# One core, four batches of attention and two expert stages: the first batch's limits on ScalarE, key high parts on GpSimd, row sums corrected with two tensor inputs

## The chip, the cores and the metric

The kernel runs on one core of a Trainium2 chip. What counts is the device time of one execution in microseconds (us). The trace is of one execution, read by the hardware profiler: TensorE (PE for its matmuls, PEld for its weight loads), VectorE (DVE), ScalarE (ACT), GpSimd (POOL), and SyncE (SP), which here issues nearly all DMAs.

## What is computed

Three layers follow each other. The change touches the first one alone: attention in which only the scores within `tau` of a row's peak are kept.

```python
scores = scale * q @ k.T                          # 4 batches, 8 heads, 576 x 576, head_dim 64
thresh = max(scores, -1) - tau
scores = where(scores >= thresh, scores, -1e9)
attn   = exp(scores - max(scores, -1))
attn   = attn / (sum(attn, -1) + 1e-9)
x      = attn @ v                                 # then heads side by side: (4, 576, 512)
h = x.T @ U @ V;  u = x + h.T                     # token mixing of rank 32
y = u + relu(u @ w_ch1) @ w_ch2                   # channel layer, 512 -> 2048 -> 512
out = routed experts of y                         # 8 experts, each token to one of them
```

## The kernel before

Attention is done batch by batch and, within a batch, by pairs of heads (4 pairs). `load_pair` (line 261) brings a pair's queries and keys in pieces named `raw`. A key piece is split into a high part `kh` (line 289, a rounding copy on ScalarE) and a low part `kl` (line 290, piece minus `kh`), so that two matmuls, lines 313 and 315, make one precise product. The pieces of queries become `qs` (line 292 on ScalarE, the low rows by line 294 on VectorE). `kl` is made on GpSimd for the three later pairs of batch 0 and for all of batch 1, otherwise on VectorE; that is the variable `eng` of line 271.

The 576 rows of the two heads are cut into groups, nine score tiles of 128 x 576 for a pair, 36 for a batch. A tile goes through these steps:

- scores into one of two PSUM tiles (TensorE, lines 313 and 315)
- the row's negated peak (VectorE, line 348, `peak`)
- `exp` of the scores, biased with the peak (ScalarE, line 359)
- the limit, peak minus tau, one number for each row (VectorE, line 352, `limits`; in batch 0 for one tile at a time, 128x1, in the later batches for two, 128x2)
- the mask: scores at or over the limit, times `exp`, with the row sum as a second result in `rv` (VectorE, line 363); it is the last reader of the PSUM tile

A group's probabilities are then turned by TensorE (line 416) and copied out of PSUM by ScalarE (line 417), multiplied with the values, and a chain of small steps (`chain`, from line 447) applies the row sums and the token mixing. `inverse` (line 378) adds 1e-9 to the row sums and takes the reciprocal. In batch 0 it is called on four sums at a time, or one; later on two, or one.

In batch 0 attention runs alone (`attention_alone`, line 553), beside a first few steps of `convert`, which turns the channel weights from 64-bit into 32-bit floats (line 212 on ScalarE, line 219 on VectorE). From batch 1 on, attention of a batch runs beside the channel layer of the one before (lines 702 to 722), whose weights are split into `w0h`, `w0l`, `w1h`, `w1l`: for batch 0's channel pass on GpSimd (lines 678 and 681) but for the first two blocks' high parts.

The order of instructions on each engine comes from a scheduler, not from the text alone; only GpSimd's instructions of batch 0's own code keep their order as written. An engine runs its queue in order: an instruction that waits holds up all behind it.

Of the kernel before, what the change touches and what calls it, by code (L numbers as in the profile page):

```python
# [14 lines left out]
AF = mybir.ActivationFunctionType  # L15
ALU = mybir.AluOpType
# [87 lines left out]
def attention_channel_moe(ctx, tc, qk, vv, tau, umat, vrep, wch, wgl, wexp, consts, out):  # L104
    nc = tc.nc
    pe, dve, act, pool, sp = nc.tensor, nc.vector, nc.scalar, nc.gpsimd, nc.sync
# [10 lines left out]
    t8 = cp.tile([128, 4], F32, name="t8")  # L117
# [135 lines left out]
    def scalars():  # L253

        sp.dma_start(out=t8[:, 0:1], in_=tau)

        dve.tensor_scalar(out=t8[:, 1:2], in0=t8[:, 0:1], scalar1=NEGTAU, scalar2=0.125, op0=ALU.is_ge, op1=ALU.mult)
        dve.tensor_scalar(out=t8[:, 2:3], in0=t8[:, 1:2], scalar1=0.0, scalar2=BIG, op0=ALU.is_equal, op1=ALU.mult)
        dve.tensor_scalar(out=t8[:, 0:1], in0=t8[:, 0:1], scalar1=0.0, scalar2=t8[:, 2:3], op0=ALU.max, op1=ALU.add)

    def load_pair(b, hp, later=None):

        i = b * NPAIR + hp
        v = ap.tile([128, VW], F32, tag="v", name=f"v{i}")
        qs = ap.tile([128, QKW], F32R, tag="qs", name=f"qs{i}")
        kh = ap.tile([128, QKW], F32R, tag="kh", name=f"kh{i}")
        kl = ap.tile([128, QKW], F32R, tag="kl", name=f"kl{i}")

        cuts = ((0, 0, 128), (1, 0, S), (0, 704, 832), (1, S, QKW), (0, 128, 704), (0, 832, QKW)) if i == 0 else (
            (1, 0, S), (1, S, QKW), (0, 0, 608), (0, 608, QKW))  # L270
        eng = dve if i == 0 or b > 1 else pool
        def steps():
            for n, (kq, c0, c1) in enumerate(cuts):
                c = slice(c0, c1)
                nm = f"raw{i}_{n}"
                if (i, n) == (0, 1):
                    x = mlp.tile([128, S], F32, tag="yr", name=nm, bufs=2)
                elif i == 0 and c1 - c0 == 128:
                    x = mlp.tile([128, 512], F32, tag="wr", name=nm, bufs=WR)
                else:  # L280
                    x = ap.tile([128, 640], F32, tag="raw", name=nm, bufs=3)
                x = x[:, :c1 - c0]
                sp.dma_start(out=x, in_=qk[i][:, kq, c])
                if (i, n) == (0, 0):
                    scalars()
                if (i, n) == (0, 3):
                    sp.dma_start(out=cst, in_=consts)
                if kq:
                    act.activation(kh[:, c], x, AF.Copy)
                    eng.tensor_tensor(out=kl[:, c], in0=x, in1=kh[:, c].bitcast(F32), op=ALU.subtract)  # L290
                else:
                    act.activation(qs[:, c], x, AF.Copy, scale=t8[:, 1:2])
                    lo, hi, xl = qs[64:128, c], qs[64:128, c].bitcast(F32), x[64:128]
                    dve.scalar_tensor_tensor(out=lo, in0=xl, scalar=t8[64:128, 1:2], in1=hi,
                                             op0=ALU.mult, op1=ALU.subtract)
                yield
            sp.dma_start(out=v, in_=vv[i])

        if later is None:
            for _ in steps():  # L300
                pass
        else:
            later.append(steps())
        return qs, kh, kl, v
# [13 lines left out]
    class Group:  # L318
# [30 lines left out]

        def limits(self, c0, c1):  # L350

            dve.tensor_scalar(out=self.st[:, 1, c0:c1], in0=self.st[:, 0, c0:c1], scalar1=-1.0, scalar2=t8[:, 0:1],
                              op0=ALU.mult, op1=ALU.subtract)

        def halves(self, h):
            return self.pt[:, h].rearrange("p (a b) -> p a b", a=2)
# [9 lines left out]
        def norm(self):  # L366

            g = self.key[2]
            rv = self.rvs[:, g, 0:self.nh]
            if self.b >= SCALED:  # L370
                inverse(rv)
                for h in range(self.nh):
                    act.activation(self.pt[:, h], self.pt[:, h], AF.Copy, scale=rv[:, h:h + 1])  # L373
            elif g == 4:
                inverse(rv)
                sp.dma_start(out=self.rvs[:64, 4, 1:2], in_=self.rvs[64:, 4, 0:1])

    def inverse(x):
        dve.tensor_scalar(out=x, in0=x, scalar1=1e-9, scalar2=None, op0=ALU.add)
        dve.reciprocal(out=x, in_=x)  # L380

    def front(b, hp, g, inp):
# [64 lines left out]
    def chain(nm, hp, half, xT, xu, rvs):  # L447
# [8 lines left out]
        if rvs is not None:  # L456
            inverse(rvs[:, c0:c0 + 2])
# [917 lines left out]
```

## Time and profile before

| | us |
|---|---|
| median of 3 runs | 1030.57 |
| lowest and highest of them | 1028.63, 1031.76 |
| profiled execution, its own time | 1029.61 |
| its span | 1027.8 |

| engine | busy us | share of the span |
|---|---|---|
| PE | 995.2 | 97% |
| PEld | 836.2 | 81% |
| DVE | 719.3 | 70% |
| ACT | 611.8 | 60% |
| POOL | 152.2 | 15% |

The busy shares are means over stages that differ: batch 0's attention fills the span's first tenth, and the last three tenths are the experts. A busy PE is a modelled figure, since matmuls overlap; the idle times of an engine, and what ended them, say more. An instruction's duration can overlap the start of the next on its engine by about a tenth of a microsecond, so what it costs its engine is read from start to start.

### The profile page before, as it was taken

To read this page: it belongs to the slowest core of one execution; us is meant where nothing else is said; L and a number is where in the kernel's file an instruction comes from. 1 tells how busy PE (TensorE), PEld (TensorE's weight loads), DVE (VectorE), ACT (ScalarE), POOL (GpSimd) and SP (SyncE) were. 2 spreads that over 40 slices of the span, in tenths; PEclk is the share of its full clock that TensorE was granted. 3 is DMA by queue.
4 is the path that set the end of the run, shared out by engine and by line. 5 is a ranking of instruction groups with operands and counts; after the bars stand their busy time and mean duration, and the time that the engine had idled before them with its cause. 6 is when DMAs were issued, how large, how long until landed. Compare 5 with 4: busy or idle time off the path is not lost. (4 is left out here: it accounts for less than half of the span.)

```text
span 1027.8 us, 17859 instructions
## 1 busy us (share of the span) xinstructions
PE 995.2 (97%) x6352; PEld 836.2 (81%) x6352; DVE 719.3 (70%) x1761; ACT 611.8 (60%) x1242; POOL 152.2 (15%) x143
## 2 busy tenths in 40 slices
PE   7898999989999999999999999999999999999996
PEld 4666677768787787788889898999998998889984
DVE  7998697776778877877676664683369755566673
ACT  6888777776677777776565653422354444455562
POOL 1332245342000000000000000013400321120100
PEclk9999999999999999999999999999999999999998
DMA  6655577864323322423121110453055555566550
GB/s 213 220 153 162 160 257 245 273 209 140 116 92 94 125 72 83 127 90 94 55 68 42 42 43 31 139 207 122 25 192 180 177 202 185 174 192 198 196 184 16
DMA packets 58241, 143.72 MB, mean 140 GB/s; under 512 B 7389, under 2 KB 8157, under 8 KB 58144
## 3 DMA queue, kind: packets, MB, share of 16 engines
q1 hardware_dynamic: 54784, 132.27, 40.0%
q0 software_dynamic: 3360, 10.23, 3.1%
q8 instruction: 52, 0.85, 0.3%
q14 instruction: 45, 0.37, 0.1%
HBM read 124.65 MB, written 18.61 MB: 139 GB/s over the span
## 5 line engine op out<-in xcount | busy, mean ns | idle before, releaser
L1125 ACT ACTIVATE eh<-ew 128x512 fp32r<-128x512 f32 x160 | 94.2, 628 | 68.1 <-PE el L1241 47.7
L1126 DVE TENSOR_TENSOR el<-ew,eh 128x512 fp32r<-128x512 f32 x160 | 106.7, 692 | 37.7 <-ACT eh L1125 36.2
L702 PE MATMUL l<-uh,w0h 128*128 128x256 f32 (+2 forms) x352 | 127.0, 361 | 0.3 <-ACT yT L508 0.3
L363 DVE SCALAR_TENSOR_TENSOR p<-s,st,p 128x576 f32<-128x576 f32 x144 | 114.1, 814 | 15.8 <-ACT p L359 12.4
L359 ACT ACTIVATE p<-s,st 128x576 f32<-128x576 f32 x144 | 103.7, 738 | 33.1 <-DVE st L348 31.6
L703 PE MATMUL l<-ul,w0h 128*128 128x256 f32 (+2 forms) x352 | 122.6, 348 | 0.0
L704 PE MATMUL l<-uh,w0l 128*128 128x256 f32 (+2 forms) x352 | 122.3, 348 | 0.0
L348 DVE TENSOR_REDUCE st<-s 128x1 f32<-128x576 f32 x144 | 105.1, 749 | 18.0 <-PE s L315 17.4
L717 PE MATMUL l<-hh,w1h 128*128 128x512 f32 (+3 forms) x320 | 115.2, 360 | 0.0
L719 PE MATMUL l<-hh,w1l 128*128 128x512 f32 (+3 forms) x320 | 112.8, 353 | 0.0
L718 PE MATMUL l<-hl,w1h 128*128 128x512 f32 (+3 forms) x320 | 112.2, 351 | 0.0
L417 ACT ACTIVATE ptt<-tp 128x512 f32<-128x512 f32 (+1 forms) x192 | 88.4, 490 | 30.1 <-PE tp L416 30.0
L313 PE MATMUL s<-kh,qs 128*128 128x288 f32 x320 | 95.5, 318 | 5.6 <-DVE p L363 3.6
L681 POOL TENSOR_TENSOR w1l<-wr,w1h 128x512 fp32r<-128x512 f32 x24 | 31.7, 1333 | 457.5 <-DVE rha L984 426.6
L416 PE MATMUL tp<-cst,p 128*128 128x128 f32 x576 | 90.8, 276 | 5.2 <-ACT ptt L417 5.0
L722 DVE TENSOR_TENSOR yT<-l,yT 128x448 f32<-128x448 f32 (+2 forms) x96 | 50.0, 521 | 57.9 <-PE l L719 57.5
L315 PE MATMUL s<-kl,qs 128*128 128x288 f32 x320 | 88.5, 296 | 0.0
L373 ACT ACTIVATE p<-p,rv 128x576 f32<-128x576 f32 x108 | 78.6, 771 | 15.3 <-DVE rv L380 15.0
L416 PEld LDWEIGHTS tp<-cst,p 128*128 128x128 f32 x576 | 67.8, 140 | 20.6 <-ACT ptt L417 11.4
L313 PEld LDWEIGHTS s<-kh,qs 128*128 128x128 f32 x320 | 60.3, 188 | 15.6 <-DVE p L363 6.4
L435 PE MATMUL po<-ptt,v 128*64 128x256 f32 (+1 forms) x256 | 69.8, 413 | 2.4 <-ACT ptt L424 1.5
L706 DVE SCALAR_TENSOR_TENSOR hl<-l,hh 128x512 fp32r<-128x512 f32 (+2 forms) x80 | 46.3, 578 | 36.7 <-ACT hh L705 36.4
(604 smaller groups left out, 2468.6 us busy)
## 6 DMA issues: line engine op xcount, KB each, us to landing
ew<-in_wexp_dram SPq DMA_DIRECT2D x80, 512.0 KB, 4.6
wr<-wdram SPq DMA_DIRECT2D x128, 256.0 KB, 3.1
cr<-in_wch_dram SPq DMA_DIRECT2D x32, 512.0 KB, 5.2
raw<-in_qk_dram SPq DMA_DIRECT2D x30, 304.0 KB, 3.2
wdram<-w SPq DMA_DIRECT2D x32, 256.0 KB, 3.0
v<-in_vv_dram SPq DMA_DIRECT2D x16, 352.0 KB, 3.9
raw<-in_qk_dram SPq DMA_DIRECT2D x16, 320.0 KB, 3.8
raw<-in_qk_dram SPq DMA_DIRECT2D x17, 288.0 KB, 3.0
```

What stands on the lines that cost most here:

```text
L313: pe.matmul(s["t"][:, h, :288], lhsT=qs[:, qc:qc + 128], rhs=kh[:, k0:k0 + 288], start=(j == 0), stop=False)
L348: dve.tensor_reduce(out=self.st[:, 0, h:h + 1], in_=self.t[h], axis=AX.XY, op=ALU.max, negate=True)
L359: act.activation(self.halves(h), self.t[h], AF.Exp, bias=self.st[:, 0, h:h + 1])
L363: dve.scalar_tensor_tensor(out=p, in0=self.t[h], scalar=self.st[:, 1, h:h + 1], in1=p, op0=ALU.is_ge, op1=ALU.mult, accum_out=self.rvs[:, ...
L416: pe.transpose(tp[:, c - c0], src[:, c * 128:c * 128 + 128], ident)
L702: pe.matmul(pm, lhsT=w1h[:, wk], rhs=uh[k], start=(k == 0), stop=False)
L703: pe.matmul(pm, lhsT=w1h[:, wk], rhs=ul[k], start=False, stop=False)
L704: pe.matmul(pm, lhsT=w1l[:, wk], rhs=uh[k], start=False, stop=(k == 3))
L717: pe.matmul(pm, lhsT=w2h[:, wd], rhs=xh, start=(f == f0), stop=False)
L718: pe.matmul(pm, lhsT=w2h[:, wd], rhs=xl, start=False, stop=False)
L719: pe.matmul(pm, lhsT=w2l[:, wd], rhs=xh, start=False, stop=(f == f0 + 3))
L1126: dve.tensor_tensor(out=lo, in0=x, in1=hi.bitcast(F32), op=ALU.subtract)
```

## The change

Three edits. `limits` of batch 0 becomes an ACTIVATE on ScalarE (out = -1 * in + bias, with the negated tau in a new column of `t8`, which costs one more small instruction in `scalars`). The copy into `kh` goes to GpSimd wherever `kl` is made there. `inverse` of an even number of sums uses an instruction that takes the sums as two tensor inputs and a maximum of (sum + 1e-9) and the sum.

```diff
+        dve.tensor_scalar(out=t8[:, 3:4], in0=t8[:, 0:1], scalar1=-1.0, scalar2=None, op0=ALU.mult)
...
-                    act.activation(kh[:, c], x, AF.Copy)
+                    if eng is pool:
+                        pool.tensor_copy(kh[:, c], x)
+                    else:
+                        act.activation(kh[:, c], x, AF.Copy)
...
         def limits(self, c0, c1):
-            dve.tensor_scalar(out=self.st[:, 1, c0:c1], in0=self.st[:, 0, c0:c1], scalar1=-1.0, scalar2=t8[:, 0:1],
-                              op0=ALU.mult, op1=ALU.subtract)
+            if self.b == 0:
+                act.activation(self.st[:, 1, c0:c1], self.st[:, 0, c0:c1], AF.Identity, scale=-1.0, bias=t8[:, 3:4])
+            else:
+                dve.tensor_scalar(out=self.st[:, 1, c0:c1], in0=self.st[:, 0, c0:c1], scalar1=-1.0, scalar2=t8[:, 0:1],
+                                  op0=ALU.mult, op1=ALU.subtract)
...
     def inverse(x):
-        dve.tensor_scalar(out=x, in0=x, scalar1=1e-9, scalar2=None, op0=ALU.add)
+        if x.free_size() % 2:
+            dve.tensor_scalar(out=x, in0=x, scalar1=1e-9, scalar2=None, op0=ALU.add)
+        else:
+            dve.scalar_tensor_tensor(out=x, in0=x, scalar=1e-9, in1=x, op0=ALU.add, op1=ALU.max)
         dve.reciprocal(out=x, in_=x)
```

The scheduler also reorders what stands around these instructions. Three places show how. The names carry batch, pair and group (`p0_2_2` is batch 0, pair 2, group 2; `raw2` and `kh2` are the third pair's), and a running number at their end that differs between the two kernels. Line numbers of the changed kernel are up to ten higher.

VectorE in batch 0, the peaks, limits and masks of one group. Before:

```order
L348 TENSOR_REDUCE st0_2_2_751<-s0_2_2_0_752 128x1
L379 TENSOR_SCALAR rv0_2_0_632<-rv0_2_0_632 128x4
L352 TENSOR_SCALAR st0_2_2_751<-st0_2_2_751,t8_63 128x1
L348 TENSOR_REDUCE st0_2_2_751<-s0_2_2_1_778 128x1
L465 TENSOR_TENSOR xsd0_0_1_364<-tx0_1_4_770,rv0_1_0_343 128x256
L363 SCALAR_TENSOR_TENSOR p0_2_2_750,rv0_2_0_632<-s0_2_2_0_752,st0_2_2_751,p0_2_2_750 128x576
L352 TENSOR_SCALAR st0_2_2_751<-st0_2_2_751,t8_63 128x1
L380 RECIPROCAL rv0_2_0_632<-rv0_2_0_632 128x4
L348 TENSOR_REDUCE st0_2_3_821<-s0_2_3_0_822 128x1
L363 SCALAR_TENSOR_TENSOR p0_2_2_750,rv0_2_0_632<-s0_2_2_1_778,st0_2_2_751,p0_2_2_750 128x576
```

The same place on VectorE now:

```order
L352 TENSOR_REDUCE st0_2_2_752<-s0_2_2_0_753 128x1
L389 SCALAR_TENSOR_TENSOR rv0_2_0_633<-rv0_2_0_633 128x4
L390 RECIPROCAL rv0_2_0_633<-rv0_2_0_633 128x4
L352 TENSOR_REDUCE st0_2_2_752<-s0_2_2_1_779 128x1
L370 SCALAR_TENSOR_TENSOR p0_2_2_751,rv0_2_0_633<-s0_2_2_0_753,st0_2_2_752,p0_2_2_751 128x576
L475 TENSOR_TENSOR xsd0_0_1_365<-tx0_1_4_771,rv0_1_0_344 128x256
L352 TENSOR_REDUCE st0_2_3_822<-s0_2_3_0_823 128x1
L370 SCALAR_TENSOR_TENSOR p0_2_2_751,rv0_2_0_633<-s0_2_2_1_779,st0_2_2_752,p0_2_2_751 128x576
```

The two limits are gone from VectorE, and the reciprocal stands nearer to its correction.

ScalarE at the same group. Before:

```order
L359 ACTIVATE p0_2_2_750<-s0_2_2_0_752,st0_2_2_751 128x576
L417 ACTIVATE ptt0_2_0_790<-tp0_2_0_0_791 128x4x128
L475 ACTIVATE xsd0_0_1_364<-tx0_1_4_770,rv0_1_0_343 64x64 x2
L417 ACTIVATE ptt0_2_0_790<-tp0_2_0_4_808 128x4x128
L359 ACTIVATE p0_2_2_750<-s0_2_2_1_778,st0_2_2_751 128x576
```

ScalarE now:

```order
L366 ACTIVATE p0_2_2_751<-s0_2_2_0_753,st0_2_2_752 128x576
L452 ACTIVATE yT0_356<-po0_1_4_737 128x320
L357 ACTIVATE st0_2_2_752<-st0_2_2_752,t8_63 128x1
L427 ACTIVATE ptt0_2_0_791<-tp0_2_0_0_792 128x4x128
L366 ACTIVATE p0_2_2_751<-s0_2_2_1_779,st0_2_2_752 128x576
L427 ACTIVATE ptt0_2_0_791<-tp0_2_0_4_809 128x4x128
L485 ACTIVATE xsd0_0_1_365<-tx0_1_4_771,rv0_1_0_344 64x64 x2
L357 ACTIVATE st0_2_2_752<-st0_2_2_752,t8_63 128x1
```

Each limit is a queue entry of ScalarE now, here with one and with three other instructions between it and its `exp`.

GpSimd at the third and fourth pairs' keys. Before:

```order
L290 TENSOR_TENSOR kl2_453<-raw2_0_454,kh2_452 128x576
L290 TENSOR_TENSOR kl2_453<-raw2_1_488,kh2_452 128x640
L681 TENSOR_TENSOR w0l0_0_1355<-wr0_0_0_1352,w0h0_0_1354 128x512
L681 TENSOR_TENSOR w1l0_0_1361<-wr0_0_1_1358,w1h0_0_1360 128x512
L290 TENSOR_TENSOR kl3_719<-raw3_0_720,kh3_718 128x576
L290 TENSOR_TENSOR kl3_719<-raw3_1_760,kh3_718 128x640
```

GpSimd now:

```order
L291 CAST kh2_453<-raw2_0_455 128x576
L294 TENSOR_TENSOR kl2_454<-raw2_0_455,kh2_453 128x576
L291 CAST kh2_453<-raw2_1_489 128x640
L294 TENSOR_TENSOR kl2_454<-raw2_1_489,kh2_453 128x640
L291 CAST kh3_719<-raw3_0_721 128x576
L691 TENSOR_TENSOR w0l0_0_1356<-wr0_0_0_1353,w0h0_0_1355 128x512
L294 TENSOR_TENSOR kl3_720<-raw3_0_721,kh3_719 128x576
L291 CAST kh3_719<-raw3_1_761 128x640
L294 TENSOR_TENSOR kl3_720<-raw3_1_761,kh3_719 128x640
L691 TENSOR_TENSOR w1l0_0_1362<-wr0_0_1_1359,w1h0_0_1361 128x512
```

Each key piece is two instructions of GpSimd in a row now, and the fourth pair's stand ahead of the second weight block.

## Rows read from the trace of the kernel before

**Rows 1.** Stretches: engine busy us (instructions): PE, PEld, DVE, ACT, POOL; PEclk, DMA share, GB/s.

```profile
8.00:99.00 91.00, 79.09 (x548) 56.88 (x546) 84.38 (x201) 73.50 (x152) 25.13 (x20) 1.00 0.61 184
99.00:260.00 161.00, 152.97 (x922) 117.78 (x922) 123.73 (x262) 118.80 (x230) 59.91 (x59) 1.00 0.66 212
260.00:1028.00 768.00, 756.49 (x4868) 658.72 (x4866) 508.93 (x1292) 415.86 (x856) 65.52 (x58) 1.00 0.37 119
```

**Rows 2.** Waits from 8 to 99 us: total us, times, longest.

```profile
DVE st L348 <- PE s L315: 4.6, 7, 1.2
DVE p L363 <- ACT p L359: 1.2, 2, 0.9
...
PE s L313 <- DVE p L363: 2.8, 4, 2.2
```

**Rows 3.** VectorE's groups, 8 to 99 us: busy us, mean ns | idle before.

```profile
L363 DVE SCALAR_TENSOR_TENSOR p<-s,st,p 128x576 f32<-128x576 f32 x36 | 29.1, 812 | 1.7 <-ACT p L359 1.2
L348 DVE TENSOR_REDUCE st<-s 128x1 f32<-128x576 f32 x36 | 26.7, 751 | 4.9 <-PE s L315 4.6
L219 DVE SCALAR_TENSOR_TENSOR w<-cr,top 128x512 int32<-128x512 int32 x7 | 7.6, 1085 | 0.0
L294 DVE SCALAR_TENSOR_TENSOR qs<-raw,t,qs 64x608 fp32r<-64x608 f32 x8 | 7.5, 936 | 0.3
L352 DVE TENSOR_SCALAR st<-st,t 128x1 f32<-128x1 f32 x36 | 7.1, 209 | 0.3
L379 DVE TENSOR_SCALAR rv<-rv 128x4 f32<-128x4 f32 x8 | 3.5, 444 | 0.1
```

**Rows 4.** Timeline of batch 0: start us, us, engine, line.

```profile
53.10 0.74 ACT L359 ACTIVATE p<-s,st 128x576 f32<-128x576 f32 x1
53.65 0.33 DVE L352 TENSOR_SCALAR st<-st,t 128x1 f32<-128x1 f32 x2
53.96 0.82 DVE L363 SCALAR_TENSOR_TENSOR p<-s,st,p 128x576 f32<-128x576 f32 x1
...
82.61 0.21 DVE L352 TENSOR_SCALAR st<-st,t 128x1 f32<-128x1 f32 x1
82.74 0.75 DVE L348 TENSOR_REDUCE st<-s 128x1 f32<-128x576 f32 x1
```

**Rows 5.** ScalarE's groups, 8 to 99 us.

```profile
L359 ACT ACTIVATE p<-s,st 128x576 f32<-128x576 f32 x36 | 26.4, 737 | 4.0 <-DVE st L348 3.7
L417 ACT ACTIVATE ptt<-tp 128x512 f32<-128x512 f32 x29 | 16.9, 596 | 2.8 <-PE tp L416 2.8
...
L289 ACT ACTIVATE kh<-raw 128x640 fp32r<-128x640 f32 x5 | 3.7, 738 | 0.6 <-DMA raw<-in_qk_dram 0.6
L289 ACT ACTIVATE kh<-raw 128x576 fp32r<-128x576 f32 x5 | 3.4, 681 | 1.4 <-issue 0.8 <-POOL w1l L681 0.6
L475 ACT ACTIVATE xsd<-tx,rv 64x64 f32<-64x64 f32 x6 | 1.5, 301 | 1.3 <-DVE xsd L465 1.3
```

**Rows 6.** GpSimd's copy of a weight block, 8 to 99 us.

```profile
L678 POOL CAST w1h<-wr 128x512 fp32r<-128x512 f32 x1 | 0.6, 612 | 15.9 <-DMA wr<-wdram 15.9
```

**Rows 7.** Timeline: VectorE's instructions with GpSimd idle, and beside GpSimd's.

```profile
56.82 0.85 DVE L294 SCALAR_TENSOR_TENSOR qs<-raw,t,qs 64x608 fp32r<-64x608 f32 x1
...
59.36 0.68 DVE L219 SCALAR_TENSOR_TENSOR w<-cr,top 128x512 int32<-128x512 int32 x1
...
61.13 1.28 POOL L681 TENSOR_TENSOR w0l<-wr,w0h 128x512 fp32r<-128x512 f32 x1 [5.80 <-ACT w0h L680]
...
61.53 1.52 DVE L294 SCALAR_TENSOR_TENSOR qs<-raw,t,qs 64x608 fp32r<-64x608 f32 x1
...
64.82 0.16 DVE L379 TENSOR_SCALAR rv<-rv 128x4 f32<-128x4 f32 x1
...
74.25 2.95 POOL L290 TENSOR_TENSOR kl<-raw,kh 128x576 fp32r<-128x576 f32 x2 [3.85 <-ACT kh L289]
...
74.49 1.21 DVE L379 TENSOR_SCALAR rv<-rv 128x4 f32<-128x4 f32 x1
```

## The prediction

> **What bounds the kernel now.** The stretches of the span come first [rows 1], since the three edits act in batch 0 and a little in batch 1. From 260 us on TensorE is busy for 756.5 of 768 us and no instruction there changes but the correction of the row sums, so that part only moves as a whole. From 99 to 260 us TensorE is busy for 153.0 of 161 us. From 8 to 99 us, batch 0's attention, it is busy for 79.1 of 91 us, while VectorE is busy for 84.4, ScalarE for 73.5 and GpSimd for 25.1. So batch 0 hangs on VectorE, the kernel after it on TensorE, and what batch 0 gains should reach the end.
>
> The waits of that stretch come next [rows 2]. VectorE waits little: 4.6 us in seven waits for a score tile, and 1.2 us in two for an `exp`. TensorE waits 2.8 us for masks, which free the two PSUM tiles. This is a loop of scores, peak, `exp`, mask, and back to scores. Then the groups of VectorE [rows 3]: 36 masks of 0.81 us, 36 peaks of 0.75, 36 limits of 0.21, and some forty others, which are not part of the loop.
>
> The sum is made against the profiled execution, 1029.61 us with a span of 1027.8, which lies 0.96 us under the median of 1030.57 that I predict for. I move that median by the sum.
>
> **Limits leave VectorE.** The 36 limits show 7.1 us, but durations overlap. Where another independent instruction follows, the next one starts 0.13 us later (82.61 to 82.74, [rows 4]). Twenty of the 36 stand so, 20 x 0.13 = 2.6 us. The other 16 stand in front of a mask or of a wait, singly or in twos; the pair at 53.65 has its mask at 53.96 [rows 4], 0.31 us later, so a limit costs between 0.15 and 0.31 there; near the pair, 16 x 0.19 = 3.0 us. VectorE's queue gets shorter by 5.6 us.
>
> Not all of it becomes time. At the pair, the `exp` started at 53.10 for 0.74 us and was over at 53.84, 0.12 before the mask [rows 4]. With the limit behind it on ScalarE the mask can't start before 53.84 plus that limit. The nearest small ACTIVATE with a factor for each row is the 64x64 of line 475, 0.30 us [rows 5]; with one column I take 0.2, and the mask would start at about 54.04, no earlier than now. So of the 3.0 us I keep a quarter, 0.8, for the places where the new order puts a mask or a correction in between, and all of the 2.6: a gain of 3.4. The bounds are 5.6 us and, with every mask 0.25 later, below nothing (the second rival).
>
> **Limits on ScalarE.** They add 36 x 0.2 = 7.2 us (10.8 at line 475's 0.30). Line 289 leaves ten times before 99 us, five of 0.74 and five of 0.68, 7.1 us [rows 5]. So ScalarE stays where it is, at 73.5 of 91 us (77 by the upper price), below VectorE. What the sum hides is the place in the queue: in seven of the 36 cases the changed order has other instructions between an `exp` and its limit, as in the excerpt with group 2 of pair 2. There a copy of 0.60 (line 417) and two of 0.30 (line 475) come first [rows 5], 1.2 us; VectorE has a mask, a product and a peak to do meanwhile, some 1.8 us, against `exp`, those three and the limit, 0.7 + 1.2 + 0.2 = 2.1. That is 0.3 late. I take 0.5 us for all seven, between 0 and 7 x 0.6 = 4.2.
>
> The extra instruction in `scalars` is a 128x1 one, 0.21 us like a limit [rows 3], at a time when VectorE waits for the first keys: 0, at most 0.2.
>
> **Key high parts on GpSimd.** The copy of 512 columns takes 0.61 us there [rows 6], so 576 take 0.69 and 640 take 0.77 by columns; ten before 99 us are 7.3 us, and GpSimd goes from 25.1 to 32.4 of 91 us, far from a bound. A key piece becomes two instructions in series, but its scores come a pair later, ten us and more: 0.
>
> The price lies elsewhere. GpSimd's work stops certain instructions of VectorE. The correction of four sums takes 0.16 us alone, but 1.21 when GpSimd has just begun `kl` (74.25 and 74.49), and an instruction with two tensor inputs, line 294, takes 0.85 alone and 1.52 beside GpSimd (61.13 and 61.53) [rows 7]. Against their undisturbed 0.68, 0.85 and 0.16 us [rows 7] the groups of lines 219, 294 and 379 [rows 3] lost 7 x 0.41 + 8 x 0.09 + 8 x 0.28 = 5.8 us, in 25.1 us of GpSimd work, 0.23 us for one. The 7.3 us more cost VectorE 7.3 x 0.23 = 1.7 us. Bounds: 0, if they meet nothing, and 5 if half of ten copies and their now later `kl` each hold a 1 us instruction.
>
> **The correction with two inputs.** If it no longer stopped behind GpSimd, it would give back the 8 x 0.28 = 2.3 us. But line 294 is of the same kind of instruction, with two tensors in SBUF, and does stop [rows 7]. So I take 0; bounds a gain of 2.3 and a loss of 0.3. The Trainium skill (SBUF — State Buffer, "Who interferes with whom") says so too: a VectorE instruction with two SBUF inputs contends with a GpSimd instruction that reads SBUF, as does a one-input one in a two-port mode, which an even count allows. By that rule this edit trades one reason to stop for another and the sum stays as it is; were the rule wrong for four elements, the sum would be 2.3 us lower. The trace has no four-element instruction of the new form.
>
> **Batch 1.** Four copies go to GpSimd there, 2.9 us of 161, beside 59.9 of GpSimd's and 118.8 of ScalarE's [rows 1]. At 0.23 that is 0.7 us on VectorE, which is busy for 123.7 and not the bound. I take 0.2.
>
> **Sum.** -3.4 + 0.5 + 1.7 + 0 + 0.2 = -1.0 us, 1029.6.
>
> **The rivals.** *VectorE's full gain.* If the masks find their limits ready, because VectorE always has other work between peak and mask, the whole 5.6 us is gained, less the 1.7: -3.9, 1026.7; with the correction freed too, -6.2, 1024.4. For it: VectorE is busy 93% of the stretch, and waits for `exp` only twice [rows 2]. Against it: the mask at 53.96 had 0.12 us to spare [rows 4].
>
> *The limit becomes the wait: slower.* Each mask hangs on `exp` and a limit in series, so the loop is longer by what is exposed. All 36 at 0.25 are 9.0, less 5.6, plus 1.7: +5.1 us, 1035.7; with the seven crowded ones at 0.6 some 1038. It decides in the mask's wait: exposure of 5.6 - 1.7 = 3.9 us, 0.11 for a tile, eats the gain. For it: two PSUM tiles only, and TensorE already waits for masks [rows 2]. Against: most waits of VectorE are for scores.
>
> *Nothing arrives.* VectorE's time is given back as waits for scores, because TensorE's own queue (79.1 of 91 us, [rows 1]) sets when they are done: 0, 1030.6.
>
> **How the numbers follow.** The forecast (1028 to 1031) has a chance of 0.40, the full gain 0.30, the slower one 0.20, nothing 0.10. About 0.3%, 3.1 us, is what a measurement of this kernel can tell from no change. Below 1027.5 lies the full gain and a little of the forecast: faster 0.32. Above 1033.7 lie most of the slower cases: 0.18. The rest, 0.50, is the same. The range runs from 1024.0, the full gain with the correction free, to 1034.0, which leaves out the worse half of the slower ones.
>
> **What would show it.** In the profile after: batch 0's last mask about 1 us earlier; VectorE's waits for ScalarE's line of limits between 0.5 and 2 us in total (over 4: the slower rival; near 0 with the stretch 4 us shorter: the full gain); the new limit at 0.2 us; corrections of four sums that still show over 0.5 us beside GpSimd; lines 219 and 294 (298 after) with a higher mean. The prediction is wrong if batch 1's time changes by more than 1 us, or if limits on ScalarE take 0.3 and more.

## The result and the profile after

The changed kernel takes 1039.41 us (median of 4 runs, 1037.69 to 1040.72), the kernel before 1030.96 beside it. The ratio is 1.0085, 95% interval 1.0071 to 1.0100: 8.5 us slower. The forecast of 1029.6 lies 9.8 us too low, and its range ended at 1034.0. The profiled execution took 1040.72 us, with a span of 1038.9 (before 1027.8).

The stretches of [rows 1], now (columns: stretch, its length, busy us of PE, PEld, DVE, ACT and POOL with counts, TensorE's granted clock, DMA share, GB/s):

```profile
8.00:99.00 91.00, 76.59 (x491) 55.27 (x492) 73.00 (x151) 67.93 (x162) 28.06 (x25) 0.91 0.58 184
99.00:260.00 161.00, 150.14 (x909) 113.95 (x910) 123.60 (x255) 113.88 (x225) 66.82 (x64) 1.00 0.63 205
```

VectorE, which the prediction took for batch 0's bound, was busy for 84.4 us of the first stretch and is now busy for 73.0, and the stretch got longer. All engines but GpSimd do less in the same 91 us. The clock was 1.00 there and is 0.91 now.

Where the time goes is read best from the masks, since each of the 144 tiles has one and their order is unchanged. Batch 0's last mask started at 98.09 us and starts at 106.46 (8.4 later). The first ones of batch 1 are 8.1 later, its last is 11.3 later (256.79 to 268.04), and from there to the end the distance stays 11.2 to 11.3. So batch 0 costs 8 us, batch 1 another 3, the rest nothing.

The waits of batch 0, 8 to 108 us (waiting engine and line, what it waited for: us in total, times, longest):

```profile
DVE st L352 <- PE s L319: 11.8, 16, 1.5
PE s L317 <- DVE p L370: 6.7, 4, 2.4
PE idle L595 <- ACT ptt L427: 4.6, 2, 4.1
ACT qs L296 <- DMA raw<-in_qk_dram: 3.8, 3, 2.3
DVE p L370 <- ACT st L357: 3.2, 5, 1.7
```

Against [rows 2]: VectorE's waits for scores went from 4.6 to 11.8 us, TensorE's for masks from 2.8 to 6.7. The new wait of masks for limits is 3.2 us. The largest single loss lies between the 18th and 19th mask, which start at 56.76 and 63.41 us; before, they started at 53.96 and 55.30. The timeline there, GpSimd, SyncE, ScalarE, VectorE, TensorE (start, us, engine, line, instruction, and in brackets the idle time ahead with what ended it):

```profile
54.19 0.66 POOL L291 CAST kh<-raw 128x576 fp32r<-128x576 f32 x1 [14.40 <-PE s L317]
54.81 1.27 POOL L691 TENSOR_TENSOR w0l<-wr,w0h 128x512 fp32r<-128x512 f32 x1
56.04 1.97 POOL L294 TENSOR_TENSOR kl<-raw,kh 128x576 fp32r<-128x576 f32 x1
58.04 2.60 SPq L284 DMA_DIRECT2D raw<-in_qk_dram  x3
60.73 0.80 ACT L296 ACTIVATE qs<-raw,t 128x608 fp32r<-128x608 f32 x1 [2.29 <-DMA raw<-in_qk_dram]
61.44 0.72 ACT L366 ACTIVATE p<-s,st 128x576 f32<-128x576 f32 x1
61.57 1.81 DVE L298 SCALAR_TENSOR_TENSOR qs<-raw,t,qs 64x608 fp32r<-64x608 f32 x1 [1.27 <-ACT qs L296]
62.88 0.38 PE L595 MATMUL idle<-idle 128*128 128x512 bf16 x1 [4.05 <-ACT ptt L427]
63.41 0.82 DVE L370 SCALAR_TENSOR_TENSOR p<-s,st,p 128x576 f32<-128x576 f32 x1
```

A pair's keys and queries come in four pieces through three buffers named `raw`, so the second query piece can only be loaded when the first key piece is done with. On GpSimd that piece now takes a copy, a weight split that the queue holds in between, and `kl`: free at 58.0 us. The load is issued at 58.04, ScalarE, at whose head the copy of that query piece stands, waits until 60.73, and everything behind it waits too: an `exp`, the copies out of PSUM, the mask, and TensorE for 4 us. Before, ScalarE made both high parts from 51.66 us on, GpSimd had only `kl` to make, and the load was issued at 53.85:

```profile
53.85 1.84 SPq L283 DMA_DIRECT2D raw<-in_qk_dram  x2
55.74 1.79 ACT L292 ACTIVATE qs<-raw,t 128x608 fp32r<-128x608 f32 x2
```

So the load is issued 4.2 us later. Of these, 2.5 us were there when the high part was begun (51.66 before, 54.19 now; by its bracket GpSimd had been idle for 14.4 us until a score matmul was done); the other 1.7 us are the longer work on the piece, the weight split of 1.27 us in between among it. Part of the gap closes again: the 18th mask is 2.8 us later than before, the 19th 8.1, the 20th 5.8.

### The profile page after: what moved, and what is told of

It is laid out like the page before. It is cut to its first block, busy times and chain, and to the rows that moved or that the text cites. A ratio compares the mean times of both kernels' runs of the same rounds, so it can differ in the third digit from the quotient of the medians.

```text
span 1038.9 us, 17831 instructions
## 1 busy us (share of the span) xinstructions
PE 1001.0 (96%) x6351; PEld 840.1 (81%) x6352; DVE 717.5 (69%) x1726; ACT 610.5 (59%) x1264; POOL 166.5 (16%) x157
## 5 line engine op out<-in xcount | busy, mean ns | idle before, releaser
L370 DVE SCALAR_TENSOR_TENSOR p<-s,st,p 128x576 f32<-128x576 f32 x144 | 114.3, 814 | 18.6 <-ACT p L366 11.8
L317 PE MATMUL s<-kh,qs 128*128 128x288 f32 x320 | 97.9, 325 | 7.9 <-DVE p L370 7.2
L426 PE MATMUL tp<-cst,p 128*128 128x128 f32 x576 | 93.1, 280 | 3.4 <-ACT ptt L427 2.4
L426 PEld LDWEIGHTS tp<-cst,p 128*128 128x128 f32 x576 | 69.1, 142 | 23.6 <-ACT ptt L427 11.8
L445 PE MATMUL po<-ptt,v 128*64 128x256 f32 (+1 forms) x256 | 71.9, 421 | 5.7 <-ACT ptt L434 3.5
L446 PE MATMUL po<-ptt,v 128*64 128x256 f32 (+1 forms) x256 | 72.1, 421 | 0.4 <-ACT ptt L427 0.4
```

What stands on the lines that cost most here:

```text
L317: pe.matmul(s["t"][:, h, :288], lhsT=qs[:, qc:qc + 128], rhs=kh[:, k0:k0 + 288], start=(j == 0), stop=False)
L370: dve.scalar_tensor_tensor(out=p, in0=self.t[h], scalar=self.st[:, 1, h:h + 1], in1=p, op0=ALU.is_ge, op1=ALU.mult, accum_out=self.rvs[:, ...
L426: pe.transpose(tp[:, c - c0], src[:, c * 128:c * 128 + 128], ident)
```

## The experiments

The theories. **K**: the copy on GpSimd holds the raw buffers longer, and late query pieces stop ScalarE's queue. **P**: GpSimd's work stops VectorE's instructions (the prediction's lock term). **L**: limits on ScalarE lengthen the loop of two tiles. **S**: the scheduler's other order costs, not the edits.

Ratios are to the kernel before, run beside on the same chip; its median lay between 1030.0 and 1035.0 us, and one chip gave both 1029.96 and, at another time, 1034.90. The traces are of one execution each, and the three columns behind the ratio tell how much later than in [rows 1]'s trace the 20th and 36th mask (batch 0, 58.50 and 98.09 us) and the 72nd (batch 1's last, 256.79) start. These columns are coarser than the ratios: c1 and e3 cost nothing by their ratios and still stand some 2 us late in all three, so 2 us in a column need not come from the edit.

| kernel | ratio, 95% interval | 20th | 36th | 72nd |
|---|---|---|---|---|
| changed | 1.0085 [1.0071, 1.0100] | 5.8 | 8.4 | 11.3 |
| z1 changed, again | 1.0117 [1.0087, 1.0146] | 5.4 | 8.0 | 14.0 |
| f1 before, again | (one run, 1029.58 us) | 0.3 | 0.2 | -0.4 |
| e1 limits alone | 1.0075 [1.0057, 1.0093] | 5.6 | 6.4 | 6.2 |
| f4 limits of 20 tiles | 1.0029 [1.0013, 1.0046] | 1.8 | 3.2 | 2.3 |
| f3 limits, two instructions each | 1.0114 [1.0085, 1.0142] | 8.8 | 13.6 | 15.0 |
| f2 no limits in batch 0 | 1.0235 [1.0210, 1.0260], see below | -0.9 | 3.1 | 2.7 |
| e2 keys alone | 1.0085 [1.0066, 1.0104] | 4.5 | 7.5 | 10.8 |
| e4 keys of batch 1's pairs alone | 1.0061 [1.0048, 1.0074] | 1.2 | 6.1 | 10.4 |
| c1 copy behind the low part | 0.9995 [0.9980, 1.0011] | 2.1 | 2.1 | 2.0 |
| c2 copy ahead of it | 1.0055 [1.0037, 1.0073] | 3.5 | 3.8 | 9.5 |
| g1 changed, queries first | 1.0072 [1.0046, 1.0097] | 5.7 | 6.4 | 5.7 |
| g3 keys alone, queries first | 1.0080 [1.0061, 1.0099] | 3.7 | 11.0 | 12.4 |
| g2 before, queries first | 1.0003 [0.9989, 1.0017] | -1.9 | -0.2 | 0.0 |
| y1 changed, own buffer | 1.0028 [1.0010, 1.0046] | 3.8 | 7.6 | 7.0 |
| y3 keys alone, own buffer | 1.0028 [1.0012, 1.0044] | 5.2 | 7.5 | 6.3 |
| y5 limits alone, own buffer | 1.0010 [0.9993, 1.0027] | 2.9 | 3.6 | 3.1 |
| y2 before, own buffer | 1.0022 [1.0005, 1.0039] | 2.8 | 3.2 | 3.8 |
| e3 sums alone | 0.9993 [0.9983, 1.0003] | 2.2 | 2.2 | 2.3 |

**One edit at a time.** e1, e2 and e3 are the three hunks of the change, each alone on the kernel before. e4 is e2 with one condition more:

```diff
-                    if eng is pool:
+                    if eng is pool and b == 1:
```

e1: 

> Only the limits of batch 0 move to ScalarE. Theory K (the key high parts on GpSimd hold the raw buffers longer, so that the queries' copy stalls ScalarE; it makes nearly all of the 8.9 us) expects 1028 to 1032 us, between the forecast's gain of 2.9 (-3.4 and +0.5) and nothing, and no wait over 2 us for a raw load in batch 0. Theory L (the limit behind its exp lengthens the loop of two tiles, and TensorE's granted clock falls in the gaps) expects 1035 to 1040, batch 0's last mask 5 us or more later than 98.09, and a granted clock well under 1.00 between 8 and 99 us.

e2: 

> Only the key high parts of batches 0 and 1 move to GpSimd. Theory K expects 1036 to 1041 us, a gap of some 5 us in the masks near 58 to 63 us as in the changed kernel, with a raw load that lands late for the queries' copy, and batch 1 about 3 us longer. Theory L expects 1030 to 1033, not more than the forecast's +1.9 us.

e3: 

> Only the correction of an even number of sums changes. By the forecast 1030.6 (no change), bounds 1028 to 1031. Theory S (what costs is the other order that the scheduler makes of any edit, not the edit) expects a change of 2 us or more in either direction here too, and the order of batch 0 differs.

e4: 

> The key high parts go to GpSimd in batch 1 alone (four pairs, eight casts), all else as before. Theory K expects the 3 us that batch 1 lost in the changed kernel (masks 182 to 214 us): 1033 to 1034.5, with batch 0 unchanged to the last mask at 98.1. If batch 1's loss came from batch 0's lateness or from the corrections of two sums, 1030 to 1031.

The limits cost 0.75%, the keys 0.85%, and neither theory had both. The sums cost nothing, but that is no test of S: read from the traces, VectorE's order in batch 0 is in e3 the one of the kernel before, but for the changed instruction. S as a general rule falls by g2 (below), whose order on VectorE and ScalarE differs in many places of batch 0 and which costs nothing (1.0003). That another order costs something in a single case stays possible. The limits' loss is there by the 20th mask; the keys' comes in both batches. The gap in e2's masks that K expected near 58 to 63 us, some 5 us, is there with 4.1 us (58.05 to 62.15; 1.3 before), but little of it lasts: the 18th mask is 4.1 us late, the 20th 4.5. e4 was expected at 1.0025 to 1.0035 with batch 0 untouched, and cost 0.61%: 4.9 us of it already between the 20th and the 36th mask, since the first keys of batch 1 are split during batch 0. There the low rows of a query (line 297 here) stood ahead of a mask while GpSimd made `kl` from 75.40 to 78.31:

```profile
75.40 2.91 POOL L293 TENSOR_TENSOR kl<-raw,kh 128x576 fp32r<-128x576 f32 x2
76.88 2.09 DVE L297 SCALAR_TENSOR_TENSOR qs<-raw,t,qs 64x608 fp32r<-64x608 f32 x1
79.00 0.82 DVE L366 SCALAR_TENSOR_TENSOR p<-s,st,p 128x576 f32<-128x576 f32 x1
79.97 0.49 PE L316 MATMUL s<-kh,qs 128*128 128x288 f32 x1 [1.98 <-DVE p L366]
```

The instruction of 0.85 us [rows 7] took 2.09, the mask behind it came late, TensorE waited for the mask, and its granted clock from 80 to 88 us was 0.57. So P exists where it meets the path: a single trace shows this, and how much of the 4.9 us is the stop and how much the lower clock behind it, it does not tell.

**Is VectorE's queue the bound?** f1 is the kernel before once more. f2 is the kernel before without batch 0's limits (the masks take the negated peak, so its attention is another; what stands behind gets other inputs with it: 25 of the 28 us that its trace is longer come after batch 1's last mask; only batch 0's part of the trace is compared).

```diff
+            if self.b == 0:
+                return
...
-            dve.scalar_tensor_tensor(out=p, in0=self.t[h], scalar=self.st[:, 1, h:h + 1], in1=p,
+            dve.scalar_tensor_tensor(out=p, in0=self.t[h], scalar=self.st[:, 1 if self.b else 0, h:h + 1], in1=p,
```

f1: 

> The kernel before once more, for a trace taken beside the other runs. If the changed kernel alone made TensorE's clock fall, the granted clock is 1.00 from 8 to 99 us here too. If the fall near 16 to 24 us is older than the change (it stood at 0.57 and 0.62 with the sums alone and with the keys of batch 1 alone), it shows here, and the first 2 us that the changed kernel seemed to lose by mask 8 aren't the change's.

f2: 

> The kernel before without the 36 limits of batch 0: each mask there takes the negated peak instead, so the first batch's attention is another. By the forecast's term (VectorE's queue binds and gets 5.6 us shorter, of which 3.4 are kept) 3.4 to 5.6 us faster. If batch 0 is bound by the loop of scores, peak, exp, mask over two PSUM tiles and not by VectorE's queue, under 1.5 us faster or nothing, with VectorE waiting more than 4.6 us for scores.

f1 repeats the kernel before to 0.3 us in every mask of batch 0, with a clock of 1.00. f2 answers the first term of the sum: with 36 limits fewer, no mask starts more than 1.8 us earlier than before, and the last one starts 3.1 later. VectorE's waits in f2's batch 0 (8 to 102 us):

```profile
DVE st L348 <- PE s L315: 7.7, 10, 1.4
DVE p L365 <- ACT p L361: 4.9, 10, 1.4
PE s L313 <- DVE p L365: 6.2, 5, 1.7
```

VectorE's two were 4.6 and 1.2 [rows 2]: 6.8 us more waiting for 7.1 us less work. What left VectorE's queue came back as its waits, nearly in full. TensorE waited longer for masks too, 6.2 us for 2.8. One reserve: the order in f2 is another, and TensorE's granted clock was 0.84 from 16 to 24 us and 0.79 from 80 to 88 (1.00 before), so a part of these waits, and of the 3.1 us, can be the clock's; up to the 31st mask f2 is between 1.8 us ahead and 2.3 behind.

**How the limits' cost grows.** f3 has a second instruction behind each limit, f4 only the limits of each group's first tile:

```diff
+                act.activation(self.st[:, 1, c0:c1], self.st[:, 1, c0:c1], AF.Copy)
...
-            if self.b == 0:
+            if self.b == 0 and c0 == 0:
```

f3: 

> The limits alone on ScalarE, and behind each a second ACTIVATE of one column that copies it in place: the same removal from VectorE, twice the instructions between exp and mask. If the limit's time in the chain of one tile makes the loss (two tiles take turns, so 0.28 us for 36 tiles is between 5 and 10 us), another 5 to 8 us over the limits alone: 1.013 to 1.017 of before. If the loss comes from the other order or from a rare event such as the clock, the same as the limits alone within 2 us: 1.006 to 1.010.

f4: 

> Only the limits of each group's first tile (20 of the 36) on ScalarE, the others on VectorE. All 36 were at 1.0075, all 36 with two instructions at 1.0114. If the cost follows the time between exp and mask, 20/36 of it: 1.003 to 1.0055. If it comes from a few places where another order or the clock decides, any value between 0.999 and 1.009.

0.29%, 0.75%, 1.14% for 20, 36 and 72 instructions: the cost grows with them, as L has it for f4 (just below its band) and less than L had for f3. e1's waits, 8 to 108 us:

```profile
DVE st L349 <- PE s L316: 10.8, 18, 1.4
PE s L314 <- DVE p L367: 6.9, 4, 2.4
DVE p L367 <- ACT st L354: 3.6, 6, 0.8
```

A place in the chain, from e1 and then from f1, at the same tile:

```profile
15.12 0.82 DVE L367 SCALAR_TENSOR_TENSOR p<-s,st,p 128x576 f32<-128x576 f32 x1 [0.78 <-ACT st L354]
16.00 0.61 PE L314 MATMUL s<-kh,qs 128*128 128x288 f32 x1 [2.36 <-DVE p L367]
```

```profile
14.34 0.82 DVE L363 SCALAR_TENSOR_TENSOR p<-s,st,p 128x576 f32<-128x576 f32 x1 [0.24 <-ACT p L359]
15.22 0.40 PE L313 MATMUL s<-kh,qs 128*128 128x288 f32 x1 [2.18 <-DVE p L363]
```

Both matmuls wait for the first of two masks and start within 0.1 us of its end. From the end of the two peaks to that mask it is 0.61 us in f1 (13.73 to 14.34), where it waits for `exp`, and 0.79 in e1 (14.33 to 15.12), where it waits for the limit behind `exp`: 0.18 us more. The second mask starts 1.35 us behind the peaks in f1, with two `exp` back to back, and 1.60 in e1, with `exp`, limit, `exp`, limit. TensorE resumes with a matmul of 0.61 us where f1 has 0.40; its granted clock from 16 to 24 us is 0.50 in e1, 1.00 in f1.

**The keys: work, or the buffers it holds?** In c1 and c2 the high parts stay on ScalarE, and GpSimd makes an extra copy of the same size in place, behind `kl` (c1) or ahead of it (c2):

```diff
                     eng.tensor_tensor(out=kl[:, c], in0=x, in1=kh[:, c].bitcast(F32), op=ALU.subtract)
+                    if eng is pool:
+                        pool.tensor_copy(kl[:, c], kl[:, c].bitcast(F32))
```

and

```diff
+                    if eng is pool:
+                        pool.tensor_copy(kh[:, c], kh[:, c].bitcast(F32))
                     eng.tensor_tensor(out=kl[:, c], in0=x, in1=kh[:, c].bitcast(F32), op=ALU.subtract)
```

c1: 

> The kernel before (key high parts on ScalarE), and GpSimd copies each low part in place behind making it: the same eighteen casts' worth of GpSimd work as the keys' edit, but no raw buffer is held for it, and ScalarE keeps its copies. If the raw buffers make the loss of the keys' edit (theory K), within 2 us of before. If GpSimd's work beside VectorE makes it (theory P: instructions with two tensor inputs stop beside GpSimd, and a mask stands behind them), 4 us or more slower, with line 294 over 1.5 us beside the copies.

c2: 

> The kernel before, and GpSimd copies each high part in place ahead of making the low part: the same GpSimd work as in the run with the copy behind, but now each raw buffer is held 0.66 to 0.72 us longer. Theory K expects 4 to 8 us slower, and more than the copy behind by 3 us or more. Theory P expects the two alike within 2 us. If neither is slow, what costs is that ScalarE's copies left their place in its queue.

The same GpSimd work (14 copies in either, not the eighteen that c1's expectation names) costs nothing behind `kl` and 0.55% ahead of it. In c1 the finished `kl` comes later too, since the copy rewrites it, so a late key by itself isn't the price. GpSimd's work by itself isn't either: line 296 rose only to 985 ns beside c1's copies (936 before [rows 3]). The pair has a flaw in batch 0: c1 keeps the order of the kernel before on VectorE, and c2 has another, so that what c2 loses there (3.8 us, c1 2.1) can't be put to the buffers alone, nor is P excluded there: in e2 the low rows of a query (line 297) ran for 1.96 us at 56.06 us, beside GpSimd, and a mask stood right behind. In batch 1 the two orders are nearly alike, c2's loss grows by another 5.7 us, and there K stands. SyncE's load and ScalarE's copy of the second query piece of one pair, c1 first, then c2:

```profile
181.69 0.33 SPq L283 DMA_DIRECT2D raw<-in_qk_dram  x1
184.64 0.81 ACT L294 ACTIVATE qs<-raw,t 128x608 fp32r<-128x608 f32 x1 [0.35 <-DMA raw<-in_qk_dram]
```

```profile
187.66 0.33 SPq L283 DMA_DIRECT2D raw<-in_qk_dram  x1
192.06 0.80 ACT L294 ACTIVATE qs<-raw,t 128x608 fp32r<-128x608 f32 x1 [2.76 <-DMA raw<-in_qk_dram]
192.89 1.19 DVE L296 SCALAR_TENSOR_TENSOR qs<-raw,t,qs 64x608 fp32r<-64x608 f32 x1 [2.30 <-ACT qs L294]
195.34 0.82 DVE L365 SCALAR_TENSOR_TENSOR p<-s,st,p 128x576 f32<-128x576 f32 x1
```

In both, the load is issued as the first key piece's `kl` ends on GpSimd. The copy of the first query piece starts 1.78 us behind that issue in c1 (183.47) and 0.80 in c2 (188.46), so the second one has to wait; it also starts later after its own issue, 4.40 us for 2.95. The mask at 195.34 stands behind that query piece in VectorE's queue; in c1 it starts at 186.69, 8.65 us earlier, where the masks around 180 us are 5 apart. The changed kernel has the same wait at the same pair, 2.65 us at 193.59.

**Two ways to free the loads.** g1, g2 and g3 load a pair's queries ahead of its keys. y1, y2, y3 and y5 give the first key piece one of two buffers (`yr`) that stand idle until batch 0's rows are stored, so that three buffers serve three pieces:

```diff
-            (1, 0, S), (1, S, QKW), (0, 0, 608), (0, 608, QKW))
+            (0, 0, 608), (0, 608, QKW), (1, 0, S), (1, S, QKW))
```

```diff
+                elif eng is pool and (kq, c0) == (1, 0):
+                    x = mlp.tile([128, S], F32, tag="yr", name=nm, bufs=2)
```

g1: 

> The changed kernel with each later pair's two query pieces loaded ahead of its two key pieces, so that a query piece never waits for a raw buffer that GpSimd still reads of the same pair. Theory K expects ScalarE's waits for raw loads to go (3.8 us in batch 0, 2.6 in batch 1, each with more behind it), no gap of the masks at 58 to 63 us, and 3 to 7 us back: 1.002 to 1.006 of before. If the late raw pieces are only a sign of something else, 1.0085 as the changed kernel.

g3: 

> Only the keys' edit, with each later pair's two query pieces loaded ahead of its key pieces. The keys' edit alone was at 1.0085 of before. Theory K expects 1.000 to 1.005, with ScalarE's waits for raw loads under 1 us in 182 to 214 us. Theory P expects 1.006 to 1.010.

g2: 

> The kernel before with each later pair's query pieces loaded ahead of its key pieces, nothing else. A control for the run above: if the order of loads is worth something by itself (SP waits 10.5 us for raw buffers that GpSimd still reads), 0 to 2 us faster; if query pieces aren't late in the kernel before, within 0.3%.

y3: 

> Only the keys' edit, but the first key piece of each pair of batch 0's later pairs and of batch 1 is loaded into a buffer that nothing else uses until later (tag yr, two of them), so the three raw buffers serve the other three pieces and no query piece waits for a key piece of its own pair. The keys' edit alone was at 1.0085. Theory K (raw buffers held by GpSimd make the query pieces late) expects 0.998 to 1.003, ScalarE's waits for raw loads under 1 us in batch 0 and in 182 to 214 us. If the copies' lateness itself is the cause (a copy and a low part in series on GpSimd, keys late for their scores), 1.005 to 1.009.

y2: 

> The kernel before with the same own buffer for the first key piece. The control for the two others: query pieces waited 1.6 us in the kernel before, so within 0.3% by theory K, and if anything faster.

y1: 

> The changed kernel with the same own buffer. Theory K for the keys and the chain for the limits together expect what the limits cost alone, 1.005 to 1.008, with no gap of the masks at 58 to 63 us. If the keys' part isn't taken away by the buffer, 1.0085 as the changed kernel.

y5: 

> The limits alone on ScalarE (key high parts stay on ScalarE), with the own buffer for the first key piece. With both edits and the own buffer the limits cost nothing over the keys' edit (1.0028 both). Theory R (limits cost where ScalarE still carries the key copies, and nothing where these have gone to GpSimd) expects 1.007 to 1.011: the 0.75% of the limits alone on the control's 1.0022. Theory B (the own buffer takes the limits' cost away too, since late raw pieces made it) expects 1.000 to 1.004.

z1: 

> The changed kernel once more, beside the run above. 1.0085 as measured, whatever the theory, unless its loss depends on the chip; by the two edits alone (1.0075 and 1.0085) it would be 1.016 if they added up.

Queries first gave nothing back (1.0072 and 1.0080). In g3 the waits for query pieces are gone as expected, but a key piece is now the one that waits for a buffer: raw loads hold SyncE's queue from 59.29 to 66.57 us, a weight load behind them is issued at 70.07, and ScalarE waits 2.98 us for weights at 75.74. GpSimd's copies themselves waited 24.6 us for raw loads in batch 0 (11.3 in e2). It looks as if the stall moved to the next transfer; no run shows that by itself.

The own buffer gave it back: 1.0028 with the keys, 1.0022 without any edit, so the keys' 0.85% shrinks to 0.06% against the control, give or take 0.23%. The traces put this into batch 1: from the 36th to the 72nd mask e2 loses 3.3 us and y3 gains 1.2, while batch 0's last mask is 7.5 us late in both (3.2 in y2). So the buffers are shown as the cause in batch 1; for batch 0 the single traces don't show it. Between 20 and 230 us no copy of a raw piece on ScalarE waits for its load in y1, y3 or y5. The two batch 0 waits that y3 still shows (1.43 and 2.02 us, by 18 us) made its expectation of under 1 us there a miss. y1 came out below its band (1.0028 for 1.005 to 1.008), and y5 says why: with the own buffer the limits cost nothing either (1.0010), though masks wait for limits longer there, 4.4 us in all, than in e1, 3.6. Theory R, that the limits cost where ScalarE still has the key copies, falls. z1 repeats the changed kernel, with the gap of the masks at the same tiles; its 1.0117 is above the 1.0085 expected, with intervals that overlap, and the edits don't add up to 1.016. No version here is measurably faster than the kernel before.

## Why the prediction was wrong, step by step

**What bounds batch 0** is the step that failed first. VectorE's 93% was read as a bound. f2 shows that it was none: its queue lost 7.1 us of limits and gained 6.8 us of waits. Of the -3.4, nothing was left at batch 0's last mask (3.1 us later). The rival "nothing arrives" (chance 0.10) had that for this term; its reason, TensorE's own queue, is not borne out, since in f2 VectorE's wait for `exp` grew most (1.2 to 4.9 us) and TensorE waited longer for masks (2.8 to 6.2). That fits the loop of two PSUM tiles over three engines' queues in order, each waiting for another; no run takes the loop away to show it. (A small miscount without weight in the sum: VectorE has 54 instructions there outside the loop, not some forty.)

**Limits on ScalarE** were taken as +0.5. Alone they cost 0.75%, 7.8 us of 1035. The price of one was near: 0.28 to 0.31 us shown (0.2 forecast, and 0.3 named as a sign of being wrong), and 0.18 from start to start where a copy follows (54.16 to 54.34 in the changed kernel). The named meter, the masks' wait for limits, stood at 3.2 us (3.6 in e1), under the 3.9 from which the slower rival was to decide; yet the time rose, and VectorE's wait for scores rose more (4.6 before, 10.8 in e1, 11.8 in the changed kernel). The rival had the sign and not the place. That the limits' cost goes with the own buffer isn't explained by a wait that the traces show: in e1 ScalarE's waits for raw pieces after 20 us are 0.7 us or less each. How much of it is the longer chain, the other order on the engines' queues, or the clock stays open.

**Keys on GpSimd, the delay**: taken as 0, since a key's scores come a pair later. The scores did have time; the buffer that the key piece comes in had not. This term is 0.55% (c2) to 0.85% (e2, with all else that the edit does), a miss about as large as the limits'. Batch 1's part of it is shown to be the buffers'; in batch 0 the changed kernel's timeline has one such stall, and how much of the loss there it makes stays open. The kernel before gave a warning: SyncE's queue waits 23.1 us for `kl` in 8 to 110 us, a row that the prediction didn't read. It tells that the buffers are all taken, and not what that costs: in the changed kernel the same wait is 19.7 us (8 to 108).

```profile
SPq L283 <- POOL kl L290: 23.1, 8, 9.4
```

**Keys on GpSimd, the lock**: +1.7 was forecast, c1 measures 0 (-0.20% to +0.11%). A mean price for each us of GpSimd work doesn't hold: line 298 did get a higher mean in the changed kernel, as forecast (1037 ns, 936 before), line 219 a lower one (905 for 1085). What counts is, by e4's trace, whether the stopped instruction stands ahead of a mask.

**The correction**: 0 was right (0.9993). It still stops: the four-sum form took 1.02 us at 59.28 in the changed kernel, inside the `kl` of 58.76 to 60.29, and its mean in e3 is 443 ns, 444 before [rows 3]:

```profile
58.76 1.53 POOL L294 TENSOR_TENSOR kl<-raw,kh 128x640 fp32r<-128x640 f32 x1
59.28 1.02 DVE L389 SCALAR_TENSOR_TENSOR rv<-rv 128x4 f32<-128x4 f32 x1
```

The Trainium skill (SBUF — State Buffer, "Who interferes with whom") has it that a two-input instruction contends with GpSimd as well; the trace agrees.

**Batch 1**: +0.2 was forecast, and it was said that over 1 us would make the prediction wrong. It lost 2.9 us from the 36th mask to the 72nd, with the wait of 2.65 us for a query piece at 193.59 in it.

**The chances**: the slower rival had 0.20, and the range stopped at 1034.0, before the place that the rival itself gave, 1035.7 to 1038.

## What to carry to other kernels

Before moving work to another engine, ask which buffer its input sits in, who loads into that buffer next, and in whose queue that load's consumer stands; the DMA queue's own waits show whether all the buffers that take turns are already in use. A busy share of 93% is no bound until work taken away shortens the stretch: leave the work out once and see whether the time or only the waits change. An edit also changes the scheduler's order: before two kernels are compared, compare the order of their instructions, and take a pair whose order is the same for the firmer proof. In a loop whose stages are on several engines with queues in order, a step that is cheap on each engine can still cost in the chain.

## What was not expected of the hardware

One stretch of TensorE's lower clock has a price that can be read. c1 and e3 keep VectorE's order of batch 0, and f1 is the kernel before itself. In all three TensorE waits 2.18 us for a mask near 15 us. In f1 the granted clock stays at 1.00; in c1 and e3 it is 0.50, the lower level (1.2 of 2.4 GHz), in each us from 17 to 23. c1's masks are 0.2 us behind those of the kernel before at the 4th, 2.0 at the 8th, and 1.1 to 2.2 from there to the 36th; e3's stand 2.1 to 2.3 behind from the 7th on (1.3 for the 16th). The stretch from 16 to 24 us, e3 first, then f1:

```profile
16.00:24.00 8.00, 6.53 (x30) 5.29 (x31) 6.78 (x15) 5.22 (x10) 2.87 (x2) 0.57 0.49 138
```

```profile
16.00:24.00 8.00, 6.10 (x40) 4.20 (x38) 7.78 (x18) 7.46 (x14) 2.52 (x2) 1.00 0.61 178
```

The changed kernel has 0.50 there throughout, and 0.79 and 0.80 in 40 to 48 and 64 to 72 us. From the 19th mask (63.41 us) to the 23rd (73.91) its masks fell no further behind (8.1 us, then 7.7), so a fall isn't always on the path. What makes the clock fall in one trace and not in another, the rows don't show: from 8 to 16 us TensorE was busy for 5.79 us in f1, 5.59 in c1, 5.42 in the changed kernel and 5.08 in e3, but f4 had 5.79 and fell to 0.57 as well, and g1 had 5.61 and stayed at 1.00.
